# Scores of a sink-window attention: each head in its own half of the array, three products instead of four

## The chip, the cores and the metric

The kernel runs on one core of a Trainium2 chip. The engines are TensorE (PE for its matmuls, PEld for its weight loads), VectorE (DVE), ScalarE (ACT), GpSimd (POOL) and SyncE (SP, which issues all transfers here). The metric is device time in microseconds (us) of one execution. Before the change it is 691.01 us, the median of three runs (689.49 to 691.43).

## The reference

Attention with four sink positions and a window of 128, then two dense layers with a squared ReLU between them:

```python
scores = (1/sqrt(D)) * q @ k.T                     # B=4, H=8, S=768, D=64
keep   = (pos_k < n_sink) | ((rel >= 0) & (rel < window))
a      = exp(scores_kept - max) / (sum + 1e-9)
x      = (a @ v) laid out as 3072 tokens x 512
out    = (max(x @ w_in, 0) ** 2) @ w_out           # 512 -> 2048 -> 512
```

All is float32 in and out, and q and k are scaled up, so the scores are large. n_sink and window are inputs.

## The kernel before, in words

Tokens are worked in eight chunks of 384 (four batches, two halves each; NQ = 3 query blocks of 128). For each chunk there are four head pairs, so 32 pairs s = 0 to 31. `attention(s, ...)` lays down the steps of one pair: load q, k, v; scores (`score`, L477); masked reduction on VectorE (L466); exp on ScalarE (L472); reciprocal of the sums (L529, L530) and scaling on GpSimd (L537); a transposition of the probabilities; values (L726, L730). `products` (L778, L823) is the two dense layers of a chunk, 16 slices of 128 hidden units each.

A query block sees 264 keys (its own block, the one before, eight sinks), or 128 where it is the first of a sequence. One matmul loads 128 queries as weights and streams the keys.

Precision: TensorE takes F32R operands at one pass, and they carry fewer bits than F32. A number is therefore split in two parts, high and low, and products of parts are added in PSUM. The dense layers use three such products. The scores come in two kinds:

- The first eight pairs (`plain`, s < 8) multiply unsplit F32 q and k. Each head has 64 rows, head 0 in rows 0 to 63 of the array, head 1 in rows 64 to 127 (L483). The program gives each such matmul as one; the trace shows two.
- The other 24 pairs are split. For head h, `QS` holds the high part of q in 64 rows and the low part in the other 64, and `KS` holds the high part of k in all 128 rows, then the low part in all 128 rows. Two matmuls of 128 rows (L489) then add all four products. To have k in both halves of the rows it is loaded twice (`load_k`, L403), and the split is done per head: a cast of k on VectorE (L441), a subtraction on GpSimd (L446), a cast of q on ScalarE (L452) and a subtraction on VectorE (L457).

The order on every engine is fixed when the program is built. `Plan` takes all steps with an engine, a cost in us, a rank, and what they read and write, and simulates the engines: at each point it picks the step that can start first, and by rank where several can. On TensorE a step also has a mode, 0 or 1, and a change of mode adds 0.17 us to the planned cost (L126). Unsplit scores have mode 1; split scores, values and products have mode 0 (L511). Score banks come from a pool of three PSUM banks (`att`), the first layer's from two (`h`), the second's from three (`o`). The planned costs decide only the order; waits at run time are real semaphores.

Of the kernel before, what the change touches and what calls it, by code (L numbers as in the profile page):

```python
# [8 lines left out]
F32 = mybir.dt.float32  # L9
F32R = mybir.dt.float32r  # L10
# [4 lines left out]
ALU = mybir.AluOpType  # L15
# [3 lines left out]
P = 128  # L19
D = 64  # L20
NS = 8
BS = P + NS
# [23 lines left out]
def f32(ap):  # L46
    return ap.bitcast(F32)
# [107 lines left out]
def sink_window_attention_moe(  # L155
# [25 lines left out]
    with ExitStack() as fast:  # L181
# [81 lines left out]
        small = wp.tile([P, 6, 2, NQ], F32, name="small")  # L263
        sums, rcp = [small[:, i] for i in range(3)], [small[:, 3 + i] for i in range(3)]
# [13 lines left out]
        def bank(key):  # L278
            return banks[plan.got[key]]
# [80 lines left out]
        HALVES = ((0, slice(0, D), slice(D, P)), (1, slice(D, P), slice(0, D)))  # L360
# [22 lines left out]
        def attention(s, rank):  # L383
# [8 lines left out]
            if plain:  # L392
                qt, kt = ("qn", "kn") if room == 0 else (f"QS{room - 1}", f"KS{room - 1}")
            else:
                qt, kt = "qn", "kn"
            qn = lambda: sb(qt, [P, TOK], F32, f"qn_{s}")
            kn = lambda: sb(kt, [P, 2, 4, BS], F32, f"kn_{s}")
            vn, sm, rs = vns[s % 2], sums[s % 3], rcp[s % 3]
            q_cell, k_cell, v_cell, sm_cell, rs_cell = qt, kt, ("vn", s % 2), ("sm", s % 3), ("rs", s % 3)

            src = k[b, 2 * p : 2 * p + 2, :, kb0 : kb0 + nk].rearrange("h d n c -> d h (n c)")

            def load_k(a):  # L403
                h = slice(a, a + 1) if plain else slice(0, 2)
                nc.sync.dma_start(
                    out=kn()[a * D : a * D + D, h, 0:nk].rearrange("d h n c -> d h (n c)"), in_=src[:, h]
                )

            add(
                ("SP", 0.42, 2.7, 197), rank(3.2), lambda: nc.sync.dma_start(out=qn(), in_=q[b, p, :, q0 : q0 + TOK]),  # L410
                writes=[q_cell],
            )
            for a in range(2):
                add(("SP", 0.57, 4.0, 244 if not plain else 122), rank(3.2), lambda a=a: load_k(a), writes=[(k_cell, a)])
# [18 lines left out]
            KS = lambda h: sb(f"KS{h}", [P, 2, 4, BS], F32R, f"KS_{s}_{h}")  # L433
            QS = lambda h: sb(f"QS{h}", [P, TOK], F32R, f"QS_{s}_{h}")
            if not plain:
                for h, own, oth in HALVES:
                    KQ = lambda h=h: (KS(h), QS(h))
                    r = rank(2.4 - 0.5 * h)
                    add(
                        ("DVE", 0.35, "port"), r,  # L440
                        lambda h=h: nc.vector.tensor_copy(KS(h)[:, 0, 0:nk], kn()[:, h, 0:nk]),  # L441
                        reads=[(k_cell, 0), (k_cell, 1)], writes=[(f"KS{h}", 0)],
                    )
                    add(
                        ("POOL", 1.35 if nk == 4 else 1.25), r,
                        lambda h=h: nc.gpsimd.tensor_tensor(  # L446
                            KS(h)[:, 1, 0:nk], kn()[:, h, 0:nk], f32(KS(h)[:, 0, 0:nk]), op=ALU.subtract
                        ),
                        reads=[(k_cell, 0), (k_cell, 1), (f"KS{h}", 0)], writes=[(f"KS{h}", 1)],
                    )  # L450
                    add(
                        ("ACT", 0.41), r, lambda h=h, own=own: nc.scalar.copy(QS(h)[own, :], qn()[own]),  # L452
                        reads=[q_cell], writes=[f"QS{h}"],
                    )
                    add(
                        ("DVE", 0.6, "port"), r,
                        lambda h=h, own=own, oth=oth: nc.vector.tensor_tensor(  # L457
                            QS(h)[oth, :], qn()[own], f32(QS(h)[own, :]), op=ALU.subtract
                        ),
                        reads=[q_cell, f"QS{h}"], writes=[f"QS{h}"],  # L460
                    )
# [15 lines left out]
            def score(i, heads, c0, n, keys):  # L477
                cols = slice(i * P, (i + 1) * P)
                for h, key in zip(heads, keys):
                    if plain:  # L480
                        own = HALVES[h][1]
                        kf = kn()[:, h].rearrange("p n c -> p (n c)")
                        nc.tensor.matmul(  # L483
                            bank(key)[:, 0:n], qn()[own, cols], kf[own, c0 : c0 + n], start=True, stop=True
                        )
                    else:
                        flat = KS(h).rearrange("p a n c -> p a (n c)")
                        for a in range(2):
                            nc.tensor.matmul(  # L489
                                bank(key)[:, 0:n], QS(h)[:, cols], flat[:, a, c0 : c0 + n],  # L490
                                start=(a == 0), stop=(a == 1),
                            )
# [7 lines left out]
            order = [(i, (0, 1)) for i in range(NQ)] if plain else [(i, (h,)) for h in range(2) for i in range(NQ)]  # L500
            for m, (i, heads) in enumerate(order):
# [658 lines left out]
```

## Time and profile before

| what | value |
|---|---|
| runs before, us | 689.49, 691.01, 691.43 |
| profiled execution, us | 688.96 |
| its span, first to last instruction, us | 686.9 |
| mean granted TensorE clock | 0.991 |
| PE, PEld, DVE, ACT, POOL busy, us | 667.4, 581.1, 459.1, 375.0, 215.2 |
| split scores on TensorE (L489) | 288 matmuls, from 107.7 to 571.7 us |
| unsplit scores on TensorE (L483) | 96 matmuls in the trace, up to 68 us |

A busy time counts a matmul from its start to its modelled end, and matmuls overlap, so that it says how full an engine is but not what one instruction costs the next. The cost of a slot is read from distances between starts in the timeline. A row that groups instructions names line, engine, operation, output<-inputs, shapes and count, then busy time and mean ns of one, then the idle time before it. The four columns of a wait are the waiting instruction and its releaser, then the total us, the times and the longest.

### The profile page before, as it was taken

What the parts mean: (1) busy time and instruction counts of PE and PEld (TensorE: products, weight loads), DVE (VectorE), ACT (ScalarE), POOL (GpSimd) and SP (SyncE); (2) the same over time, 40 slices, a digit from 0 to 9 for tenths busy, and PEclk for the clock granted to TensorE, in tenths of its full rate; (3) what the DMA queues carried; (4) which work ended last, traced back from release to release, by engine and by line L of the source; (5) the groups of instructions that cost most, each with busy time, mean ns of one, the idle gap of its engine ahead of it and who ended that gap; (6) DMA issues with size and microseconds to landing.
All of it is one profiled execution on the core that took longest, in us unless ns stands there. A gap on an engine that the chain in (4) does not pass through costs nothing.

```text
span 686.9 us, 11380 instructions
## 1 busy us (share of the span) xinstructions
PE 667.4 (97%) x3722; PEld 581.1 (85%) x3722; DVE 459.1 (67%) x1194; ACT 375.0 (55%) x1073; POOL 215.2 (31%) x377
## 2 busy tenths in 40 slices
PE   4999989999999999999999999999999999999996
PEld 3667879998888888888888898888898888899985
DVE  7599999967987655676677766666776764242222
ACT  6798734355464434456666656666666565442221
POOL 4455433534544513232244323223332322000000
PEclk9799999999999999999999999999999999999999
DMA  7746455215777532466556666555557754310001
GB/s 244 220 163 203 168 192 183 84 52 157 223 245 227 154 106 93 134 207 193 155 148 184 211 188 201 170 167 174 145 169 213 223 160 114 116 51 12 0 1 51
DMA packets 58178, 104.78 MB, mean 153 GB/s; under 512 B 6208, under 2 KB 34624, under 8 KB 58112
## 3 DMA queue, kind: packets, MB, share of 16 engines
q1 hardware_dynamic: 58112, 103.98, 49.7%
q8 instruction: 31, 0.51, 0.3%
q14 instruction: 35, 0.29, 0.1%
HBM read 79.58 MB, written 24.38 MB: 151 GB/s over the span
## 4 chain that ended last, share of the span: by engine, by line
PE 90%; DVE 6%; ACT 1%; issue 1%; DMA 1%; SPq 0%; POOL 0%; DVEq 0%
PE bank L823 37%; PE bank L778 37%; PE bank L726 6%; PE bank L489 5%; PE bank L730 1%; DVE f L310 1%; PE bank L590 1%; PE bank L483 1%; DVE P L466 1%; PE bank L638 1%; DVE f L317 1%; DVE f L303 1%; DMA kn<-in_k_dram 1%; ACT w L323 0%; DVE w L327 0%
## 5 line engine op out<-in xcount | busy, mean ns | idle before, releaser
L778 PE MATMUL bank<-x,w 128*128 128x384 f32 x1536 | 303.1, 339 | 0.7 <-DVE gl L807 0.7
L778 PEld LDWEIGHTS bank<-x,w 128*128 128x128 f32 x1536 | 267.0, 188 | 9.5 <-issue 1.4
L823 PE MATMUL bank<-w,gh 128*128 128x512 f32 x768 | 242.7, 397 | 2.1 <-ACT ob L864 2.1
L823 PEld LDWEIGHTS bank<-w,gh 128*128 128x128 f32 x768 | 137.5, 188 | 21.4 <-ACT ob L864 2.4
L823 PE MATMUL bank<-w,gl 128*128 128x512 f32 x384 | 151.4, 394 | 0.0
L446 POOL TENSOR_TENSOR KS<-kn,KS 128x408 fp32r<-128x408 f32 (+1 forms) x48 | 64.9, 1352 | 225.1 <-DVE KS L441 164.2
L791 ACT ACTIVATE r<-bank 128x384 f32<-128x384 f32 x128 | 62.7, 490 | 129.3 <-PE bank L778 128.2
L472 ACT ACTIVATE P<-P,nbs 128x264 f32<-128x264 f32 (+1 forms) x192 | 94.4, 492 | 66.5 <-DVE nbs L466 65.7
L800 DVE TENSOR_TENSOR bank<-bank,r 128x384 f32<-128x384 f32 x128 | 72.1, 563 | 83.4 <-ACT r L791 83.1
L537 POOL TENSOR_SCALAR P<-P,small 128x128 f32<-128x128 f32 (+1 forms) x168 | 88.5, 543 | 71.1 <-DVE small L530 48.9
L823 PEld LDWEIGHTS bank<-w,gl 128*128 128x128 f32 x384 | 72.1, 188 | 16.6
L466 DVE CUSTOM_DVE_ANT_0 P<-bank,maskA 128x264 f32<-128x264 f32 x128 | 53.4, 426 | 45.1 <-PE bank L489 43.6
L807 DVE TENSOR_TENSOR gl<-bank,gh 128x384 fp32r<-128x384 f32 x128 | 70.9, 554 | 17.4 <-ACT gh L795 11.8
L795 ACT ACTIVATE gh<-r 128x384 fp32r<-128x384 f32 x128 | 66.7, 521 | 4.7 <-PE bank L823 2.2
L668 DVE STREAM_TRANSPOSE T<-P 128x384 f32<-128x384 f32 x96 | 45.2, 495 | 22.6 <-POOL P L537 21.7
L489 PEld LDWEIGHTS bank<-KS,QS 128*128 128x128 f32 x288 | 51.6, 188 | 6.2 <-DVE nbs L466 0.4
L489 PE MATMUL bank<-KS,QS 128*128 128x264 f32 (+1 forms) x288 | 55.4, 279 | 0.0
L742 ACT CAST x<-bank 128x384 fp32r<-128x384 f32 x32 | 15.3, 478 | 52.6 <-PE bank L730 52.4
L327 POOL TENSOR_TENSOR w<-f,w 128x512 fp32r<-128x512 f32 x19 | 27.1, 1430 | 51.4 <-ACT w L323 51.4
L726 PE MATMUL bank<-PT,vn 128*64 128x256 f32 (+1 forms) x392 | 40.6, 347 | 0.0
L726 PEld LDWEIGHTS bank<-PT,vn 128*64 128x64 f32 x392 | 25.7, 139 | 15.5 <-issue 6.7
L529 DVE TENSOR_TENSOR small<-small,eps 128x3 f32<-128x3 f32 (+1 forms) x56 | 34.5, 616 | 3.3 <-ACT P L472 2.7
(90 smaller groups left out, 575.5 us busy)
## 6 DMA issues: line engine op xcount, KB each, us to landing
raw<-in_moe_w_dram SPq DMA_DIRECT2D x32, 512.0 KB, 3.7
half<-in_moe_w_dram SPq DMA_DIRECT2D x64, 256.0 KB, 3.6
via<-T SPq DMA_DIRECT2D x48, 192.0 KB, 3.7
PT<-via SPq DMA_DIRECT2D x12, 768.0 KB, 4.4
via<-T SPq DMA_DIRECT2D x48, 160.0 KB, 4.2
PT<-via SPq DMA_DIRECT2D x12, 640.0 KB, 4.7
kn<-in_k_dram SPq DMA_DIRECT2D x24, 272.0 KB, 4.4
qn<-in_q_dram SPq DMA_DIRECT2D x32, 192.0 KB, 3.6
```

The costliest lines, as they stand in the source:

```text
L446: lambda h=h: nc.gpsimd.tensor_tensor(KS(h)[:, 1, 0:nk], kn()[:, h, 0:nk], f32(KS(h)[:, 0, 0:nk]), op=ALU.subtract),
L466: nc.vector.tensor_tensor_reduce(Pt(h)[:, i, o : o + n], ps_[:, 0:n], mask[:, 0:n], -SCALE, BIG, ALU.add, ALU.min, nb)
L472: nc.scalar.activation(Pt(h)[:, i, o : o + n], Pt(h)[:, i, o : o + n], AF.Exp, bias=nb, scale=-1.0, accum_out=sm[:, h, i : i + 1],)
L489: nc.tensor.matmul(bank(key)[:, 0:n], QS(h)[:, cols], flat[:, a, c0 : c0 + n], start=(a == 0), stop=(a == 1),)
L537: {"POOL": nc.gpsimd, "DVE": nc.vector}[engine].tensor_scalar(a, a, rs[:, h, i : i + 1], 1.0, op0=ALU.mult, op1=ALU.mult)
L726: nc.tensor.matmul(xo[h * D : h * D + D, qs[0] * P : qs[0] * P + len(qs) * P], vn[:, kk, h, :], rhs(), start=(n == 0), stop=False, skip_gr ...
L778: nc.tensor.matmul(bank(key)[:, 0:TOK], wi[fc][:, i, cc * P : (cc + 1) * P], xt[:, cc, :], start=(cc == 0 and j == 0), stop=(cc == NCC - 1 ...
L791: lambda key=key, r=r: nc.scalar.activation(r(), bank(key)[:, 0:TOK], AF.Relu),
L795: ("ACT", 0.41), n - 9, lambda gh=gh, r=r: nc.scalar.activation(gh(), r(), AF.Square),
L800: lambda key=key, r=r: nc.vector.tensor_tensor(bank(key)[:, 0:TOK], bank(key)[:, 0:TOK], r(), op=ALU.mult),
L807: lambda key=key, gh=gh, gl=gl: nc.vector.tensor_tensor(gl(), bank(key)[:, 0:TOK], f32(gh()), op=ALU.subtract),
L823: nc.tensor.matmul(bank(okey), gt()[:, ts_], wo[f][:, i, :], start=(f == f0 and j == 0), stop=(f == f1 - 1 and j == 2),)
```

## The change

Split scores keep each head in its own 64 rows, as the unsplit ones do. `QS` and `KS` become two tiles of two parts, `[:, 0]` high and `[:, 1]` low, with head 0 in rows 0 to 63 and head 1 in rows 64 to 127. k is loaded once into 128 rows, and q and k of both heads are split in one pass each. A query block's scores are three products for each head (q high with k high, q high with k low, q low with k high), the two heads alternating, in two PSUM banks. Both heads then go through one reciprocal step, and their transpositions have one rank. Split pairs get two buffers of their own for incoming q and k (`qns`, `kns`); the first kind uses one of them and the two parts of `QS` and `KS` as its three rooms.

```diff
+        qns = [wp.tile([P, TOK], F32, name=f"qn{i}") for i in range(2)]
+        kns = [wp.tile([P, 4, BS], F32, name=f"kn{i}") for i in range(2)]
...
-            for a in range(2):
-                add(("SP", 0.57, 4.0, 244 if not plain else 122), rank(3.2), lambda a=a: load_k(a), writes=[(k_cell, a)])
+            add(
+                ("SP", 0.5, 4.0, 70 * nk), rank(3.2),
+                lambda: nc.sync.dma_start(out=kn[:, 0:nk].rearrange("d n c -> d (n c)"), in_=src), writes=[k_cell],
+            )
...
-            KS = lambda h: sb(f"KS{h}", [P, 2, 4, BS], F32R, f"KS_{s}_{h}")
-            QS = lambda h: sb(f"QS{h}", [P, TOK], F32R, f"QS_{s}_{h}")
+            QS = lambda a: sb("QS", [P, 2, TOK], F32R, "q_parts")[:, a]
+            KS = lambda a: sb("KS", [P, 2, 4, BS], F32R, "k_parts")[:, a]
...
+                    ("DVE", 0.35, "port"), r, lambda: nc.vector.tensor_copy(KS(0)[:, 0:nk], kn[:, 0:nk]),
...
+                    lambda: nc.gpsimd.tensor_tensor(
+                        KS(1)[:, 0:nk], kn[:, 0:nk], f32(KS(0)[:, 0:nk]), op=ALU.subtract
+                    ),
...
+                    ("ACT", 0.41), r, lambda: nc.scalar.copy(QS(0), qn), reads=[q_cell],
...
+                    lambda: nc.vector.tensor_tensor(QS(1), qn, f32(QS(0)), op=ALU.subtract),
...
-                    else:
-                        flat = KS(h).rearrange("p a n c -> p a (n c)")
-                        for a in range(2):
-                            nc.tensor.matmul(
-                                bank(key)[:, 0:n], QS(h)[:, cols], flat[:, a, c0 : c0 + n],
-                                start=(a == 0), stop=(a == 1),
-                            )
+                ks = (kn,) if plain else (KS(0), KS(1), KS(0))
+                qs = (qn,) if plain else (QS(0), QS(0), QS(1))
+                for j, (qj, kj) in enumerate(zip(qs, ks)):
+                    kf = kj.rearrange("p n c -> p (n c)")
+                    for h, key in zip(heads, keys):
+                        own = slice(h * D, h * D + D)
+                        nc.tensor.matmul(
+                            bank(key)[:, 0:n], qj[own, cols], kf[own, c0 : c0 + n],
+                            start=(j == 0), stop=(j == len(qs) - 1),
+                        )
...
-            order = [(i, (0, 1)) for i in range(NQ)] if plain else [(i, (h,)) for h in range(2) for i in range(NQ)]
-            for m, (i, heads) in enumerate(order):
+            heads = (0, 1)
+            for i in range(NQ):
...
-                    reads, cost = [f"QS{h}", (f"KS{h}", 0), (f"KS{h}", 1)], (0.245 if n > P else 0.17)
+                    reads, cost = [(x, a) for x in ("QS", "KS") for a in range(2)], (0.4 if n > P else 0.23)
                 add(
                     ("PE", cost, 1 if plain else 0), r,
...
-            groups = ((0, 1),) if plain else ((0,), (1,))
-            for heads in groups:
+            if True:
...
                 for h in range(2):
-                    r = rank(1.3 if not plain and h == 0 else 0.9)
+                    r = rank(0.95)
```

How the order moves, at two places. First TensorE in the middle of the program, the scores of pair 20. Before, the three blocks of head 0 and then those of head 1 stand singly between products; these are the second block of head 0 and what is around it (x00 and x10 are the high and low part of the attention output, KS_20_0 and QS_20_0 the split operands of head 0):

```order
L778 MATMUL bank3_70<-x00_138,w_18_1060 128x384 x2
L778 MATMUL bank3_70<-x10_139,w_18_1060 128x384
L489 MATMUL bank2_69<-KS_20_0_3327,QS_20_0_3321 128x264 x2
L778 MATMUL bank3_70<-x00_138,w_18_1060 128x384 x2
L778 MATMUL bank3_70<-x10_139,w_18_1060 128x384
```

In the changed program the first block of the same pair (`score` is now L479, the products L765 and L810; k_parts and q_parts are the split operands of both heads):

```order
L810 MATMUL bank6_73<-w_15_957,gh_1_579 128x512 x2
L810 MATMUL bank6_73<-w_15_957,gl_1_589 128x512
L479 MATMUL bank2_69<-k_parts_959,q_parts_824 128x264
L479 MATMUL bank0_67<-k_parts_959,q_parts_824 128x264
L479 MATMUL bank2_69<-k_parts_959,q_parts_824 128x264
L479 MATMUL bank0_67<-k_parts_959,q_parts_824 128x264
L479 MATMUL bank2_69<-k_parts_959,q_parts_824 128x264
L479 MATMUL bank0_67<-k_parts_959,q_parts_824 128x264
L810 MATMUL bank5_72<-w_15_957,gh_1_579 128x512 x2
L810 MATMUL bank5_72<-w_15_957,gl_1_589 128x512
```

Six groups of two for a pair have become three groups of six. The whole order has 72 such groups, and each stands between products or transpositions that use the full array.

Second VectorE, behind the scores of the same pair. Before, the transpositions of head 0 stand among the reductions of head 1:

```order
L668 STREAM_TRANSPOSE T_20_3564<-P_20_0_3478 128x3x4x32
L466 ISA P_20_1_3547,nbs_125<-bank2_69,maskA_84 128x264
L466 ISA nbs_125 128x1
L668 STREAM_TRANSPOSE T_20_3564<-P_20_0_3478 128x2x4x32
L672 STREAM_TRANSPOSE T_20_3564<-P_20_0_3478 128x4x32
L466 ISA P_20_1_3547,nbs_125<-bank1_68,maskA_84 128x264
```

In the changed program those of both heads stand together (L787 and L794 belong to the products):

```order
L794 TENSOR_TENSOR gl_1_589<-bank3_70,gh_1_579 128x384
L655 STREAM_TRANSPOSE T_20_3498<-P_20_0_3371 128x3x4x32
L655 STREAM_TRANSPOSE T_20_3498<-P_20_0_3371 128x2x4x32
L659 STREAM_TRANSPOSE T_20_3498<-P_20_0_3371 128x4x32
L655 STREAM_TRANSPOSE T_20_3498<-P_20_1_3373 128x3x4x32
L655 STREAM_TRANSPOSE T_20_3498<-P_20_1_3373 128x2x4x32
L659 STREAM_TRANSPOSE T_20_3498<-P_20_1_3373 128x4x32
L734 TENSOR_TENSOR x11_145<-bank2_69,x01_144 128x384
L787 TENSOR_TENSOR bank4_71<-bank4_71,r_0_542 128x384
```

All six transpositions of a pair now follow one another, with the next product's L787 behind them.

More of the change, by code (lines that the diff above doesn't have):

```diff
@@ L431, in attention @@
                 Pt, P_cell = (lambda h: sb(f"P{h}", [P, NQ, BAND], F32, f"P_{s}_{h}")), (lambda h: ("P", h))
-            KS = lambda h: sb(f"KS{h}", [P, 2, 4, BS], F32R, f"KS_{s}_{h}")
-            QS = lambda h: sb(f"QS{h}", [P, TOK], F32R, f"QS_{s}_{h}")
+            QS = lambda a: sb("QS", [P, 2, TOK], F32R, "q_parts")[:, a]
+            KS = lambda a: sb("KS", [P, 2, 4, BS], F32R, "k_parts")[:, a]
             if not plain:
[L436 to L461, printed above, removed]
@@ new lines, in attention @@
+                first = s == NPS
+                r = rank(2.4)
+                add(
+                    ("DVE", 0.35, "port"), r, lambda: nc.vector.tensor_copy(KS(0)[:, 0:nk], kn[:, 0:nk]),
+                    reads=[k_cell], writes=[("KS", 0)] + [("KS", 1)] * first,
+                )
+                add(
+                    ("POOL", 1.35 if nk == 4 else 1.25), r,
+                    lambda: nc.gpsimd.tensor_tensor(
+                        KS(1)[:, 0:nk], kn[:, 0:nk], f32(KS(0)[:, 0:nk]), op=ALU.subtract
+                    ),
+                    reads=[k_cell, ("KS", 0)], writes=[("KS", 1)],
+                )
@@ L463, in reduce_ @@
+                add(
+                    ("ACT", 0.41), r, lambda: nc.scalar.copy(QS(0), qn), reads=[q_cell],
+                    writes=[("QS", 0)] + [("QS", 1)] * first,
+                )
+                add(
+                    ("DVE", 0.5, "port"), r,
+                    lambda: nc.vector.tensor_tensor(QS(1), qn, f32(QS(0)), op=ALU.subtract),
+                    reads=[q_cell, ("QS", 0)], writes=[("QS", 1)],
+                )
             def reduce_(h, i, n, o, mask, key):
@@ L554, in part_sinks @@
                     )
-            groups = ((0, 1),) if plain else ((0,), (1,))
-            for heads in groups:
-                hs = slice(heads[0], heads[-1] + 1)
-                r = rank(1.05 if plain or heads[0] else 1.45)
+            if True:
+                r = rank(1.05)
                 add(
-                    ("DVE", 0.22), r - URGE, lambda hs=hs: recip(hs),
+                    ("DVE", 0.22), r - URGE, lambda: recip(slice(0, 2)),
                     reads=[("e", s, h, i) for h in heads for i in range(NQ)], writes=[(rs_cell, h) for h in heads],
```

34 lines of the change are left out of this document (12 added, 22 removed).

## The prediction

> **What bounds the kernel now.** I read the page's busy shares first, then its chain, then the busy time by stage, the waits of TensorE in the long middle stage, and last the timeline of TensorE, because the question turns out to be what one group of matmuls costs there. From the page:
>
> ```profile
> PE 667.4 (97%) x3722; PEld 581.1 (85%) x3722; DVE 459.1 (67%) x1194; ACT 375.0 (55%) x1073; POOL 215.2 (31%) x377
> PE 90%; DVE 6%; ACT 1%; issue 1%; DMA 1%; SPq 0%; POOL 0%; DVEq 0%
> ```
>
> The four stages, each row with the busy time of PE, PEld, DVE, ACT and POOL, the granted clock and the DMA share; then the only wait of TensorE's matmuls between 107 and 572 us:
>
> ```profile
> 0.00:28.00 28.00, 17.48 (x91) 12.17 (x92) 17.77 (x81) 18.38 (x61) 13.92 (x38) 0.82 0.77 238
> 28.00:107.00 79.00, 76.64 (x467) 61.20 (x465) 75.53 (x169) 57.62 (x149) 34.28 (x46) 1.00 0.55 184
> 107.00:572.00 465.00, 464.30 (x2609) 411.05 (x2608) 330.84 (x869) 261.24 (x772) 165.15 (x288) 1.00 0.56 168
> 572.00:687.00 115.00, 108.95 (x562) 96.69 (x560) 35.01 (x78) 37.76 (x95) 1.88 (x5) 0.99 0.15 47
> PE bank L778 <- DVE gl L807: 0.7, 1, 0.7
> ```
>
> All split scores run from 107 to 572 us. There TensorE is idle for 0.7 us of 465 and waits once. VectorE is at 71%, GpSimd at 36%. So in this stage the time is the number of TensorE slots times their length, and a faster VectorE, ScalarE, GpSimd or DMA returns at most that 0.7 us. Everything the change does to TensorE's stream there goes into the end, one for one.
>
> **What a slot costs now.** Busy times overlap between matmuls, so I go by distances between starts. The timeline of TensorE, several places (start, length, instruction, count; a row merges neighbours):
>
> ```profile
> 203.42 0.41 PE L489 MATMUL bank<-KS,QS 128*128 128x264 f32 x2
> 203.66 0.68 PE L778 MATMUL bank<-x,w 128*128 128x384 f32 x3
> 209.88 2.27 PE L778 MATMUL bank<-x,w 128*128 128x384 f32 x12
> 211.99 0.39 PE L823 MATMUL bank<-w,gh 128*128 128x512 f32 x1
> 291.30 0.63 PE L823 MATMUL bank<-w,gh 128*128 128x512 f32 x2
> 291.77 0.39 PE L823 MATMUL bank<-w,gl 128*128 128x512 f32 x1
> 297.27 0.33 PE L489 MATMUL bank<-KS,QS 128*128 128x128 f32 x2
> 297.44 0.68 PE L823 MATMUL bank<-w,gh 128*128 128x512 f32 x2
> 297.96 0.39 PE L823 MATMUL bank<-w,gl 128*128 128x512 f32 x1
> L489 PE MATMUL bank<-KS,QS 128*128 128x264 f32 x240 | 48.0, 285 | 0.0
> L489 PE MATMUL bank<-KS,QS 128*128 128x128 f32 x48 | 8.1, 249 | 0.0
> ```
>
> Twelve first products take 211.99 - 209.88 = 2.11 us, 0.176 each. Two score matmuls of 264 columns take 203.66 - 203.42 = 0.24, 0.12 each. Two of 128 columns take 0.17, and the two L823 behind them 0.52 instead of 0.47: 0.22 for both, 0.11 each. The 288 score matmuls are 72 query blocks (24 head pairs of three) with four each, 60 blocks of 264 columns and 12 of 128. A block costs 4 x 0.12 = 0.48 us, or 0.44.
>
> **What the change makes of a block.** Six matmuls of 64 rows, in three pairs, one head in each half of the array. If the halves overlap, a block has three slots instead of four: 3 x 0.12 = 0.36. The trace has such pairs: the unsplit scores L483, which also use 64 rows per head, with F32 operands. Here is what surrounds them (the last five rows are narrow windows, to part the first two matmuls from the second two, and one that shows the clock at 9 us):
>
> ```profile
> 35.45 0.71 PE L483 MATMUL bank<-kn,qn 64*128 64x264 f32 x4
> 36.10 1.31 PE L778 MATMUL bank<-x,w 128*128 128x384 f32 x6
> 37.34 0.72 PE L483 MATMUL bank<-kn,qn 64*128 64x264 f32 x4
> 37.98 0.44 PE L590 MATMUL bank<-ident,PSK 128*128 128x128 f32 x2
> 38.88 0.71 PE L483 MATMUL bank<-kn,qn 64*128 64x264 f32 x4
> 39.53 0.44 PE L726 MATMUL bank<-PTS,vn 128*64 128x128 f32 x3
> 54.31 1.85 PE L778 MATMUL bank<-x,w 128*128 128x384 f32 x9
> 56.00 0.39 PE L823 MATMUL bank<-w,gh 128*128 128x512 f32 x1
> 37.34 0.49 PE L483 MATMUL bank<-kn,qn 64*128 64x264 f32 x2
> 37.66 0.39 PE L483 MATMUL bank<-kn,qn 64*128 64x264 f32 x2
> 8.99 0.39 PE L483 MATMUL bank<-kn,qn 64*128 64x264 f32 x2
> 9.22 0.60 PE L483 MATMUL bank<-kn,qn 64*128 64x264 f32 x4
> 8.90:9.50 0.60, 0.60 (x8) 0.55 (x7) 0.60 (x7) 0.32 (x2) 0.00 (x0) 1.00 1.09 328
> ```
>
> The two heads do overlap: both first matmuls stand in one row at 37.34 and the next two start 0.32 later. Inside a run of such pairs the distance is 9.22 - 8.99 = 0.23. Going in and out costs extra, in four places:
> - Before the group. Between the groups at 35.45 and 37.34 the six L778 take 1.24 us, not 6 x 0.176 = 1.06. Of the 0.18, 0.11 belongs to the exit (next point but one); 0.07 is the entry.
> - First pair of the group: 0.32 instead of 0.23, 0.09. Its weights are loaded with nothing streaming.
> - Last pair: 37.98 - 37.66 = 0.32 instead of 0.23, 0.09, before TensorE starts what follows.
> - Behind the group: the nine L778 from 54.31, which come straight after an L483 group, take 1.69, not 1.58: 0.11, again a first weight load that nothing covers.
>
> Sum 0.36 us for one trip into the 64-row shape and back. Rows of 64 columns (L726) are another shape: from L483 straight into L726 the distance is 39.53 - 38.88 = 0.65, no less than the 0.64 into the full array, though both are F32. So the price goes with the change of shape, not with the type of number. The Trainium skill, in "TensorEngine Tiling (Array Packing)", section Key Properties, says that a change of tiling mode, not merely of tile, drains TensorE; by that rule the change loses, and the trace agrees with its 0.07 and 0.09, and adds two bare weight loads.
>
> In the changed order each of the 72 blocks stands alone between full-array matmuls: 72 trips that were not there. The planner counts such a block as 0.4 us with no change of mode (its third number is 0, where unsplit scores have 1), so nothing gathers them.
>
> **The sum.**
> - 60 blocks: 0.36 + 0.36 - 0.48 = +0.24, 14.4 us.
> - 12 blocks of 128 columns: 0.33 + 0.36 - 0.44 = +0.25; I take +0.22, since part of the first load runs beside a slot that is itself bound by loading. 2.6 us.
> - Unsplit scores: 16 runs instead of 14, two more trips, 0.7 us; three more of them now border on L726 groups and share a change, about -0.16 each, -0.5.
> - One k load instead of two at the start. TensorE's matmuls wait for kn twice, 5.1 us in all and 4.6 of it the first time, so the second half's lateness is worth at most 0.5; I take -0.2. Not in the trace: what one 128-partition load takes to land; as late as the second half now, it gains nothing.
>
> ```profile
> PE bank L483 <- DMA kn<-in_k_dram: 5.1, 2, 4.6
> PE bank L823 <- ACT ob L864: 2.1, 1, 2.1
> L441 DVE CAST KS<-kn 128x544 fp32r<-128x544 f32 x24 | 10.5, 446 | 0.0
> L446 POOL TENSOR_TENSOR KS<-kn,KS 128x544 fp32r<-128x544 f32 x24 | 35.9, 1497 | 106.3 <-DVE KS L441 63.9 <-DMA half<-in_moe_w_dram 34.1 <-DMA vn<-in_v_dram 7.4
> L457 DVE TENSOR_TENSOR QS<-qn,QS 64x384 fp32r<-64x384 f32 x48 | 30.1, 627 | 2.2 <-ACT QS L452 0.8
> L529 DVE TENSOR_TENSOR small<-small,eps 128x3 f32<-128x3 f32 x48 | 32.6, 679 | 3.3 <-ACT P L472 2.7
> ```
>
> - Splitting once per pair drops 24 passes each of L441 (0.45), L457 (0.63) and L446 (1.50 for the long form), and 24 of L529 (0.68): some 42 us of VectorE and up to 36 of GpSimd. All of it lies beside TensorE, which waits 0.7 us for VectorE in that stage. I cost it at -0.3. The same goes for half the k traffic. The 2.1 us wait at the end of the first stage (for L864, where VectorE is 96% busy) I keep; it could go or double.
>
> Together +16.7 us. The profiled execution took 688.96 us, 2.1 beyond its 686.9 span: span 703.6, execution 705.7. The median of the runs is 691.01, 2.05 above that execution, so I forecast **707.7 us**.
>
> Bounds of the block, the term that decides: a 64-row pair with the split's number type isn't in the trace. At best there is no price for the change of shape, 0.36 against 0.48, 72 x -0.12 = -8.6 us. At worst the halves do not overlap, 6 x 0.12 + 0.36 = 1.08, 72 x 0.6 = +43 us. I take the L483 value since those matmuls have the same rows, columns and neighbours.
>
> **The rivals.**
> *Faster: the shape changes free of charge.* With this number type TensorE takes 64-row pairs without emptying itself, and the third slot saved decides: -8.6, -0.5 for starts and waits, 682. The Trainium skill, in "TensorEngine Tiling (Array Packing)", section Theoretical Speedup, gives up to 2x for 64 rows, with no price named there; that is this case, and no run here shows it for the split's type. For: only F32 pairs are seen. Against: the 0.07 before a group is paid behind L778, which has the split's type. The point at which it turns is 0.12 us per trip; three times that was measured.
>
> *Half price.* The drains (0.07 + 0.09) stay, but the loads are drawn forward under the running matmuls, as in full-array work. 0.36 + 0.16 - 0.48 = +0.04 per block: 694. Against: 0.09 and 0.11 bare in every group looked at.
>
> *A new wait on top.* A block now needs two of three score banks at once, and both heads' transposes stand in one row on VectorE:
>
> ```profile
> L668 DVE STREAM_TRANSPOSE T<-P 128x384 f32<-128x384 f32 x48 | 27.5, 573 | 22.6 <-POOL P L537 21.7
> L668 DVE STREAM_TRANSPOSE T<-P 128x256 f32<-128x256 f32 x48 | 20.0, 416 | 0.0
> L672 DVE STREAM_TRANSPOSE T<-P 128x128 f32<-128x128 f32 x24 | 6.6, 274 | 0.0
> ```
>
> Six of them are 2 x (0.57 + 0.42 + 0.27) = 2.5 us in which VectorE frees no bank and makes no gl. If TensorE waits 0.5 us for that in each of 24 pairs, 12 us on top: 720. Against: blocks of a pair stand some 4 us apart in the order, VectorE loses 42 us of work, and TensorE now runs slower than the planner thinks, which leaves the others ahead.
>
> **How the numbers follow.** Forecast 0.74, faster 0.10, half price 0.08, new wait 0.08. About 0.3% (2 us) is what a measurement of this kernel can tell from no change. Forecast and new wait are slower; of half price nearly all is slower, 0.01 the same; a partly free change could land near zero, another 0.01. Slower 0.89, same 0.02, faster 0.09. The forecast's own spread is 701 to 714 (0.30 to 0.43 per trip, waits of -3 to +3). The range reaches to half price on one side and part of a new wait on the other: 696 to 715.
>
> **What would show it.** In the changed profile the stage of the split scores should last some 17 us longer with TensorE still near 100% busy. Between two full-array matmuls around a block, the block's six should start in three pairs 0.11 to 0.22 apart, and the distance from the first to the next full-array start should be near 0.55, with 0.07 lost before and 0.11 behind. VectorE should drop by some 40 us to about 420, GpSimd to about 180. The last stage, from the last score to the end, should keep its 115 us. The forecast is wrong if the first pair starts without a gap behind a product, if the two heads' starts lie a slot apart, or if TensorE waits for VectorE in the middle stage.

## The result, and the profile after

The changed kernel takes 707.46 us (median of four runs, 707.03 to 707.57), the kernel before 691.22 in the runs beside it (four, 689.49 to 692.46). The ratio is 1.0242, 95% interval 1.0218 to 1.0266: slower by 2.4%. The forecast was 707.7.

The profiled execution of the changed kernel took 707.47 us, its span is 705.6. From the page, the busy shares and the chain of the end:

```profile
PE 685.6 (97%) x3866; PEld 571.4 (81%) x3866; DVE 418.7 (59%) x1100; ACT 361.8 (51%) x1041; POOL 176.7 (25%) x359
PE 92%; DVE 5%; issue 1%; DMA 0%; ACT 0%; DVEq 0%
```

TensorE is as full as before and busy 18 us longer; VectorE lost 40 us, GpSimd 38, ScalarE 13. By stage (columns as in the prediction: length, then PE, PEld, DVE, ACT, POOL, granted clock, DMA share, GB/s), the third stage now ending at 600 us:

```profile
0.00:28.00 28.00, 17.32 (x93) 12.55 (x95) 18.26 (x81) 19.15 (x63) 14.34 (x37) 0.82 0.73 255
28.00:107.00 79.00, 76.71 (x464) 60.91 (x465) 74.10 (x172) 53.40 (x136) 35.46 (x50) 1.00 0.55 184
107.00:600.00 493.00, 492.85 (x2813) 409.95 (x2812) 296.24 (x784) 256.72 (x765) 126.90 (x272) 1.00 0.49 148
600.00:705.00 105.00, 98.71 (x501) 87.97 (x500) 30.12 (x65) 32.52 (x78) 0.00 (x0) 0.98 0.11 39
```

TensorE is idle for 0.15 us of 493 there. Split scores stand from 136.5 to 587.2 us (before 107.7 to 571.7). The waits of TensorE's matmuls, the first three from 28 to 107 us, the fourth the only one from 107 to 600, and one of its weight loads, also from 107 to 600:

```profile
PE bank L765 <- ACT x L729: 1.0, 1, 1.0
PE bank L765 <- DVE x L734: 0.7, 1, 0.7
PE bank L810 <- DVE ob L851: 0.5, 1, 0.5
PE bank L765 <- DVE gl L794: 0.2, 1, 0.2
PEld bank L479 <- issue: 21.2, 60, 0.4
```

The long wait of before (2.1 us for L864) is gone, and three shorter ones add up to 2.2. The last row is the change's own mark: before 60 of the 72 blocks the loading of weights stands still for 21.2/60 = 0.35 us, and nothing that the profile shows releases it (ahead of the other 12 it stands still as long, with some engine's name beside it). The timeline of TensorE, around a block of 128 columns and one of 264:

```profile
303.79 0.39 PE L810 MATMUL bank<-w,gl 128*128 128x512 f32 x1
304.11 0.55 PE L479 MATMUL bank<-k_parts,q_parts 64*128 64x128 f32 x6
304.59 0.73 PE L810 MATMUL bank<-w,gh 128*128 128x512 f32 x2
305.16 0.39 PE L810 MATMUL bank<-w,gl 128*128 128x512 f32 x1
309.35 0.40 PE L810 MATMUL bank<-w,gl 128*128 128x512 f32 x1
309.68 0.63 PE L479 MATMUL bank<-k_parts,q_parts 64*128 64x264 f32 x6
310.24 2.38 PE L765 MATMUL bank<-x,w 128*128 128x384 f32 x12
312.45 0.39 PE L810 MATMUL bank<-w,gh 128*128 128x512 f32 x1
```

The L810 ahead of the block of 264 takes 309.68 - 309.35 = 0.33 us instead of 0.23, the block 310.24 - 309.68 = 0.56, and the twelve L765 behind it 2.21 instead of 2.11. So the last matmul before a block pays 0.10, and the first behind it 0.10. In the median over all 72 blocks the second pair starts 0.23 after the first, the third 0.12 after the second, and the next full-array matmul 0.21 after the third.

Where all of the time went is seen best by counting, for each matmul of either trace, the time from its start to the next matmul's start, and adding these up by kind:

| from a start to the next, summed, us | before | after | difference |
|---|---|---|---|
| split scores | 34.5 | 39.7 | +5.3 |
| first layer (L778, now L765) | 276.9 | 281.4 | +4.5 |
| second layer (L823, now L810) | 269.9 | 276.8 | +7.0 |
| transposes | 22.7 | 23.3 | +0.6 |
| values, unsplit scores | 71.8 | 72.0 | +0.2 |
| first to last matmul | 675.9 | 693.4 | +17.5 |

Two thirds of the loss don't stand with the scores but with their neighbours, as 0.10 before and behind each block. Of the 18.8 us by which the span grew (686.85 to 705.62), the rest is 0.3 at the start (first matmul at 4.89, before at 4.62) and 1.0 between the start of the last matmul and the end.

### The profile page after: what moved, and what is told of

It is laid out like the page before. It is cut to its first block, busy times and chain, and to the rows that moved or that the text cites. A ratio compares the mean times of both kernels' runs of the same rounds, so it can differ in the third digit from the quotient of the medians.

```text
span 705.6 us, 11365 instructions
## 1 busy us (share of the span) xinstructions
PE 685.6 (97%) x3866; PEld 571.4 (81%) x3866; DVE 418.7 (59%) x1100; ACT 361.8 (51%) x1041; POOL 176.7 (25%) x359
## 4 chain that ended last, share of the span: by engine, by line
PE 92%; DVE 5%; issue 1%; DMA 0%; ACT 0%; DVEq 0%
PE bank L765 38%; PE bank L810 37%; PE bank L479 7%; PE bank L713 6%; PE bank L717 2%; PE bank L577 1%; PE bank L625 1%; DVE P L460 1%; DVE f L312 1%; DVE f L305 1%; DVE f L319 1%; DMA pari<-in_params_dram 0%; DVE gl L794 0%; DVE bank L787 0%; DVE VS L375 0%
## 5 line engine op out<-in xcount | busy, mean ns | idle before, releaser
L765 PE MATMUL bank<-x,w 128*128 128x384 f32 x1536 | 303.7, 342 | 1.9 <-ACT x L729 1.0
L765 PEld LDWEIGHTS bank<-x,w 128*128 128x128 f32 x1536 | 267.7, 188 | 17.9 <-ACT x L729 1.4
L810 PE MATMUL bank<-w,gh 128*128 128x512 f32 x768 | 243.5, 398 | 0.5 <-DVE ob L851 0.5
L787 DVE TENSOR_TENSOR bank<-bank,r 128x384 f32<-128x384 f32 x128 | 72.1, 563 | 154.1 <-ACT r L778 153.4
L810 PEld LDWEIGHTS bank<-w,gh 128*128 128x128 f32 x768 | 139.2, 188 | 22.4 <-DVE ob L851 0.8
L810 PE MATMUL bank<-w,gl 128*128 128x512 f32 x384 | 151.4, 394 | 0.0
L778 ACT ACTIVATE r<-bank 128x384 f32<-128x384 f32 x128 | 62.9, 491 | 127.6 <-PE bank L765 126.5
L442 POOL TENSOR_TENSOR k_parts<-kn,k_parts 128x408 fp32r<-128x408 f32 (+1 forms) x24 | 33.6, 1401 | 314.8 <-issue 285.8
L526 POOL TENSOR_SCALAR P<-P,small 128x264 f32<-128x264 f32 (+1 forms) x174 | 83.4, 503 | 50.7 <-DVE small L519 46.5
L810 PEld LDWEIGHTS bank<-w,gl 128*128 128x128 f32 x384 | 72.0, 188 | 16.5
L794 DVE TENSOR_TENSOR gl<-bank,gh 128x384 fp32r<-128x384 f32 x128 | 71.0, 555 | 13.1 <-ACT gh L782 3.5
L460 DVE CUSTOM_DVE_ANT_0 P<-bank,maskA 128x264 f32<-128x264 f32 x128 | 50.5, 428 | 30.9 <-PE bank L479 30.3
L729 ACT CAST x<-bank 128x384 fp32r<-128x384 f32 x32 | 15.3, 478 | 72.3 <-PE bank L717 72.3
L479 PEld LDWEIGHTS bank<-k_parts,q_parts 64*128 64x128 f32 x432 | 30.1, 185 | 25.6 <-issue 21.2
L655 DVE STREAM_TRANSPOSE T<-P 128x384 f32<-128x384 f32 x96 | 43.4, 490 | 11.6 <-POOL P L526 11.1
L479 PE MATMUL bank<-k_parts,q_parts 64*128 64x264 f32 (+1 forms) x432 | 44.6, 311 | 0.0
L466 ACT ACTIVATION_READ_ACCUMULATOR P<-P,nbs 128x1 f32 x192 | 36.0, 187 | 0.0
```

The lines of the kernel that those rows point to most:

```text
L460: nc.vector.tensor_tensor_reduce(Pt(h)[:, i, o : o + n], ps_[:, 0:n], mask[:, 0:n], -SCALE, BIG, ALU.add, ALU.min, nb)
L466: nc.scalar.activation(Pt(h)[:, i, o : o + n], Pt(h)[:, i, o : o + n], AF.Exp, bias=nb, scale=-1.0, accum_out=sm[:, h, i : i + 1],)
L479: nc.tensor.matmul(bank(key)[:, 0:n], qj[own, cols], kf[own, c0 : c0 + n], start=(j == 0), stop=(j == len(qs) - 1),)
L526: {"POOL": nc.gpsimd, "DVE": nc.vector}[engine].tensor_scalar(a, a, rs[:, h, i : i + 1], 1.0, op0=ALU.mult, op1=ALU.mult)
L655: nc.vector.transpose(dst.rearrange("p c j b -> p j c b"), src.rearrange("p j (c b) -> p j c b", b=32))
L765: nc.tensor.matmul(bank(key)[:, 0:TOK], wi[fc][:, i, cc * P : (cc + 1) * P], xt[:, cc, :], start=(cc == 0 and j == 0), stop=(cc == NCC - 1 ...
```

## The experiments

The theory: a block pays for leaving and entering the full-array shape, about as much as its three pairs take, and nothing else in the change matters. The rivals: the halves don't overlap; the new order or a new wait does it; the relief of the other engines was worth something and hid part of the price. A ratio is always to the kernel before, run on the same chip.

**A second trip in each block, and the same matmul with no trip.** Into the changed kernel, a small full-array matmul between the first pair and the second of each split block. It writes columns that nobody reads, but its start clears the sum of the first product, so that this product is missing from head 0's scores. The time of the other steps does not depend on it.

```diff
+                    if not plain and j == 0:
+                        nc.tensor.matmul(
+                            bank(keys[0])[:, 504:512], qj[:, cols], kf[:, 0:8], start=True, stop=True,
+                            skip_group_check=True,
+                        )
```

> The changed kernel with one more matmul in each of the 72 split blocks: 128 rows, 8 columns, between the first and the second pair of 64-row matmuls, into columns of the bank that nobody reads. Theory (the change of shape is what costs): each block makes a second trip, last pair +0.09, a bare weight load 0.11, entry 0.09, first pair +0.10, so about +0.39 us per block, 72 x 0.39 = +28 us: 735. Rival (the 64-row pairs themselves are slow, the change of shape is cheap): only one more slot of at most 0.12, +8.6 us: 716. Rival (new waits behind the scores): 708 to 716.

The control puts the same matmul, with the same loss of a product, into the kernel before, where it changes no shape:

```diff
+                            if h == 0 and a == 0:
+                                nc.tensor.matmul(
+                                    bank(key)[:, 504:512], QS(h)[:, cols], flat[:, 0, 0:8], start=True, stop=True,
+                                    skip_group_check=True,
+                                )
```

> Control on the kernel before: the same 128-row, 8-column matmul between the two score matmuls of head 0 in each of the 72 blocks, where everything is full array. Theory: it costs one slot bound by its weight load, 0.11 to 0.12 us, so +7.7 to +8.6 us: 699. If an extra tiny matmul by itself cost as much as in the changed kernel (rival: the insertion and not the shape), it would be +28: 719.

The first took 734.98 us (ratio 1.0644, 1.0613 to 1.0675), 27.5 above the changed kernel, 0.38 for each of the 72. The control took 698.25 (1.0112, 1.0083 to 1.0141), 7.8 above the kernel before, 0.11 each. The timeline of TensorE with the second trip:

```profile
320.69 0.40 PE L815 MATMUL bank<-w,gl 128*128 128x512 f32 x1
321.02 0.39 PE L479 MATMUL bank<-k_parts,q_parts 64*128 64x264 f32 x2
321.33 0.27 PE L484 MATMUL bank<-k_parts,q_parts 128*128 128x8 f32 x1
321.54 0.51 PE L479 MATMUL bank<-k_parts,q_parts 64*128 64x264 f32 x4
321.98 1.32 PE L770 MATMUL bank<-x,w 128*128 128x384 f32 x6
```

And the control's:

```profile
202.77 0.28 PE L489 MATMUL bank<-KS,QS 128*128 128x264 f32 x1
202.89 0.17 PE L494 MATMUL bank<-KS,QS 128*128 128x8 f32 x1
202.92 0.37 PE L489 MATMUL bank<-KS,QS 128*128 128x264 f32 x1
203.12 2.07 PE L783 MATMUL bank<-x,w 128*128 128x384 f32 x11
```

The block with a second trip takes 0.96 instead of 0.56 us. Its first pair takes 0.31 until the next start, where it took 0.22; the small matmul takes 0.21; and the pair behind it takes 0.22 again, as if it were the first. In the control the small matmul adds 0.11. So 0.29 of the 0.40 goes with the change of shape alone; the other 0.11 is what the same small matmul costs in the control, as much as a full-array matmul of 128 columns. The price of a trip is thus measured apart from everything else in the change. The Trainium skill, "TensorEngine Tiling (Array Packing)", section Key Properties, says that changing the mode drains TensorE; that agrees with the 0.31 of a pair that would take 0.22, and with the 0.10 ahead of a block.

**Only one of the three products.** The changed kernel with q high times k high alone, so that its scores lack the low parts:

```diff
-                ks = (kn,) if plain else (KS(0), KS(1), KS(0))
-                qs = (qn,) if plain else (QS(0), QS(0), QS(1))
+                ks = (kn,) if plain else (KS(0),)
+                qs = (qn,) if plain else (QS(0),)
```

> The changed kernel with only the first of the three products (q high with k high); the other two are left out, so the scores lack their low parts. Theory: two slots less per block and the whole trip stays, -2 x 0.12 x 60 - 2 x 0.11 x 12 = -17 us: 690.5, so that two matmuls per block cost what four full-array ones cost before. Rival (the products are what costs): two thirds of a block's measured 0.77 us go, 72 x 0.51 = -37 us: 671.

It took 690.95 us (eight runs; ratio 1.0005, 0.9994 to 1.0016). Its timeline:

```profile
302.24 0.40 PE L810 MATMUL bank<-w,gl 128*128 128x512 f32 x1
302.57 0.39 PE L479 MATMUL bank<-k_parts,q_parts 64*128 64x264 f32 x2
302.89 0.61 PE L765 MATMUL bank<-x,w 128*128 128x384 f32 x2
```

A third of the changed kernel's score matmuls, and no gain on the kernel before: the trip with one pair (0.33 - 0.23 + 0.32 + 0.10 = 0.52) costs what four full-array matmuls did. The other two pairs are (707.46 - 690.95) / 72 = 0.23 us together, 0.115 each. Inside the 64-row shape a pair costs what a full-array matmul of as many columns costs. It is the way there that isn't free.

**Whether the halves overlap, in two ways.** First, head 1's second and third products left out (its scores lack the low parts), which leaves a pair and two single matmuls:

```diff
+                        if h == 1 and j > 0:
+                            continue
...
-                            start=(j == 0), stop=(j == len(qs) - 1),
+                            start=(j == 0), stop=(j == len(qs) - 1 or h == 1),
```

> The changed kernel with head 1's second and third product left out (its scores lack their low parts); head 0 keeps three. Theory (the two halves of the array work at the same time, also where head 0's and head 1's matmuls stand apart in the program): head 0's three slots stay, 706.5 to 708. Rival (halves take turns): two slots less per block, 72 x 0.23 = -17 us: 690.

It took 707.05 us (1.0234, 1.0214 to 1.0255), 0.4 less than with all six. Its timeline:

```profile
309.16 0.63 PE L481 MATMUL bank<-k_parts,q_parts 64*128 64x264 f32 x4
309.72 0.44 PE L767 MATMUL bank<-x,w 128*128 128x384 f32 x1
```

Four matmuls take 0.56 as six did: head 1's two lay wholly beside head 0's. Second, the same six matmuls with the heads one after the other, meant to take the overlap away:

```diff
-                for j, (qj, kj) in enumerate(zip(qs, ks)):
-                    kf = kj.rearrange("p n c -> p (n c)")
-                    for h, key in zip(heads, keys):
...
+                def one(j, h, key):
+                    own = slice(h * D, h * D + D)
+                    kf = ks[j].rearrange("p n c -> p (n c)")
+                    nc.tensor.matmul(
+                        bank(key)[:, 0:n], qs[j][own, cols], kf[own, c0 : c0 + n],
+                        start=(j == 0), stop=(j == len(qs) - 1),
+                    )
+
+                for h, key in zip(heads, keys):
+                    for j in range(len(qs)):
+                        one(j, h, key)
```

> The changed kernel with the three products of head 0 first and then those of head 1, instead of alternating. Theory (halves overlap when neighbours in the stream use different halves): only the last of head 0 and the first of head 1 overlap, five slots instead of three, +2 x 0.12 x 60 + 2 x 0.11 x 12 = +17 us: 724. Rival (the halves do not really overlap in the changed kernel either): no change, 707 to 708. If the array ran both halves out of order: 707 to 708 too.

It took 708.23 us (1.0257, 1.0227 to 1.0286), not 724. The edit did reach the program: its order on TensorE has three matmuls into one bank, then three into the other. But the timeline has the block of before the edit:

```profile
309.42 0.40 PE L813 MATMUL bank<-w,gl 128*128 128x512 f32 x1
309.74 0.64 PE L478 MATMUL bank<-k_parts,q_parts 64*128 64x264 f32 x6
310.31 0.44 PE L768 MATMUL bank<-x,w 128*128 128x384 f32 x1
```

Six in 0.57 us, and their starts in the trace stand in three pairs. Within a pair they are 10 ns apart in the median over all 72 blocks, and 19 at most. In program order head 1's first matmul could start only with or after head 0's third, and the six would need five slots; they took three. So TensorE started head 1's first matmul before head 0's second, which stands ahead of it in the program. The trace does not name the bank of a start, so this is read from the distances. The Trainium skill, "TensorE: Matmul & The Clock Gate", Part 3, The mechanism, says that matmuls start and end in program order with no reordering; the starts of this run differ, and they decide here. The edit therefore didn't test what it was meant to; the one before it did.

**The order alone, and the planner's numbers.** The kernel before with nothing but the change's order: both heads of a block in one step, one reciprocal step, transposes and splits of one rank, and the planned cost of such a step (0.49 or 0.46 us). k is still loaded twice and split per head, in full-array matmuls.

```diff
-            order = [(i, (0, 1)) for i in range(NQ)] if plain else [(i, (h,)) for h in range(2) for i in range(NQ)]
+            order = [(i, (0, 1)) for i in range(NQ)]
...
-            groups = ((0, 1),) if plain else ((0,), (1,))
+            groups = ((0, 1),)
...
-                    r = rank(1.3 if not plain and h == 0 else 0.9)
+                    r = rank(0.95)
```

> The kernel before with only the order of the change: both heads of a query block in one step of four full-array matmuls, one reciprocal step for both, transpositions of one rank; k loaded twice and split per head as before. Theory (the shape is the whole loss): 690 to 692.5. Rival (both heads at once in three banks, and six transpositions in a row, make TensorE wait): 697 to 707.

And the changed kernel with a planner that knows what a block takes:

```diff
-                    reads, cost = [(x, a) for x in ("QS", "KS") for a in range(2)], (0.4 if n > P else 0.23)
+                    reads, cost = [(x, a) for x in ("QS", "KS") for a in range(2)], (0.77 if n > P else 0.68)
```

> The changed kernel with the planner told what a split block costs as measured, 0.77 and 0.68 us instead of 0.4 and 0.23; nothing else. Theory (TensorE is full, its slots set the time): 706 to 709, no change beyond 1.5 us. Rival (the loss is partly an order laid out by wrong costs): 701 to 705.

The order alone took 691.48 us (ten runs; 1.0015, 1.0004 to 1.0026), about 1 us more than the kernel before. Its timeline has the four matmuls of a block in 0.49 us, and the middle stage is as full as it was:

```profile
224.25 0.65 PE L489 MATMUL bank<-KS,QS 128*128 128x264 f32 x4
224.74 0.51 PE L778 MATMUL bank<-x,w 128*128 128x384 f32 x2
107.00:572.00 465.00, 463.64 (x2604) 410.54 (x2603) 326.73 (x820) 260.70 (x770) 156.78 (x282) 1.00 0.57 168
```

Two banks at a time and six transposes in a row make no wait worth the name, even with all of VectorE's old passes. The better planner gave 707.35 us (1.0248, 1.0231 to 1.0265): nothing. So some 15 of the 16 us are left for the shape of the matmuls, together with whatever the single load and split of k and q gave back.

**The same new layout with no change of shape.** In the changed kernel, each head's parts of q go into tiles whose other 64 rows are zero. Then six full-array matmuls do what the three pairs do; k is still loaded and split once. There is one buffer for incoming q instead of two, the split of q is two passes of half the rows each, and GpSimd clears the tiles once.

```diff
-        qns = [wp.tile([P, TOK], F32, name=f"qn{i}") for i in range(2)]
+        qns = [wp.tile([P, TOK], F32, name="qn0")]
...
+            QZ = lambda: sb("QZ", [P, 2, 2, TOK], F32R, "q_parts")
...
-                        own = slice(h * D, h * D + D)
+                        own = slice(h * D, h * D + D) if plain else slice(0, P)
+                        qj = qn if plain else QZ()[:, h, (0, 0, 1)[j]]
```

> The changed kernel with its three products per head, k loaded and split once, but q written into two tiles whose other 64 rows are zero, so that every score matmul has 128 rows: six full-array slots per block, no change of shape (and one more ScalarE and VectorE pass per pair for q; one buffer for q instead of two). Theory: 6 x 0.12 = 0.72 instead of the measured 0.77 us, 0.65 instead of 0.68 for 128 columns: -0.05 x 60 - 0.03 x 12 = -3.2 us: 704.3. Rival (the loss is waits or order, not the shape): as the changed kernel or later for the two more passes, 707 to 709.

It took 708.78 us (1.0268, 1.0251 to 1.0285), 4.5 more than the theory and within the rival's 707 to 709, so the total alone does not tell them apart. The block does; from the timeline:

```profile
305.90 0.39 PE L823 MATMUL bank<-w,gl 128*128 128x512 f32 x1
306.13 0.78 PE L492 MATMUL bank<-k_parts,q_parts 128*128 128x128 f32 x6
306.75 0.45 PE L823 MATMUL bank<-w,gh 128*128 128x512 f32 x1
```

Nothing is lost before it (0.23), and six slots take 0.62, where the changed kernel's block of 128 columns takes 0.48 and 0.20 around it. Summed over all 72 blocks with their edges this is some 52 us against some 54: of the 3.2 us expected, about 2 came. More than that was lost elsewhere, most of it early. The stage from 92 to 127 us, in this kernel and then in the changed one, and last this kernel's longest wait of TensorE there:

```profile
92.00:127.00 35.00, 33.44 (x171) 29.09 (x168) 33.87 (x58) 14.41 (x28) 11.50 (x7) 1.00 0.58 195
```

```profile
92.00:127.00 35.00, 34.55 (x174) 31.11 (x173) 33.66 (x56) 15.06 (x29) 15.12 (x10) 1.00 0.55 193
```

```profile
96.88 0.45 PE L778 MATMUL bank<-x,w 128*128 128x384 f32 x1 [1.24 <-DVE x L747]
```

VectorE is at 97 and 96%. Compared at points where both have the same matmuls of every kind behind them, the padded kernel is 0.1 us ahead of the changed one at 93 us, 1.8 behind at 100 and still 1.75 behind at 128. In between lies that wait of 1.2 us for x. Just ahead of this x VectorE does the cast of a first k (1.47 us) and one of the half passes of q (0.54); the changed kernel has its first such cast at 83.7 us, out of the way. So this part of the loss is a matter of what stands where. Whether the added passes or the missing buffer moved it was not tried apart. What the run does show: in full-array matmuls six slots cost almost what the three pairs and their trip do.

**Whether the passes that the change saves were worth nothing.** The changed kernel with each of the four splitting passes done twice, the second writing the same again (one of the four is shown):

```diff
+def twice(emit):
+    emit()
+    emit()
...
-                    ("DVE", 0.35, "port"), r, lambda: nc.vector.tensor_copy(KS(0)[:, 0:nk], kn[:, 0:nk]),
+                    ("DVE", 0.35, "port"), r, lambda: twice(lambda: nc.vector.tensor_copy(KS(0)[:, 0:nk], kn[:, 0:nk])),
```

> The changed kernel with each of the four passes that split q and k of a pair done twice, so that VectorE, GpSimd and ScalarE get back the passes the change took from them (24 more of each). Theory (they lie beside a full TensorE): 706.5 to 709. Rival (the relief returned part of a larger loss): 710 to 716.

And once more, with a planner that knows it:

```diff
-                    ("DVE", 0.35, "port"), r, lambda: twice(lambda: nc.vector.tensor_copy(KS(0)[:, 0:nk], kn[:, 0:nk])),
+                    ("DVE", 0.9, "port"), r, lambda: twice(lambda: nc.vector.tensor_copy(KS(0)[:, 0:nk], kn[:, 0:nk])),
...
-                    ("POOL", 1.35 if nk == 4 else 1.25), r,
+                    ("POOL", 3.0 if nk == 4 else 2.5), r,
...
-                    ("ACT", 0.41), r, lambda: twice(lambda: nc.scalar.copy(QS(0), qn)), reads=[q_cell],
+                    ("ACT", 1.0), r, lambda: twice(lambda: nc.scalar.copy(QS(0), qn)), reads=[q_cell],
...
-                    ("DVE", 0.5, "port"), r,
+                    ("DVE", 1.2, "port"), r,
```

> The split passes done twice as in the run before, but now the planner is told their doubled lengths (0.9 and 1.2 us on VectorE, 3.0 or 2.5 on GpSimd, 1.0 on ScalarE), so that the order allows for them. Theory (the passes fit beside TensorE, and the 14 us came from an order that put scores where their operands were late): 706.5 to 710. Rival (the engines' time itself is short): 715 to 722.

The first took 721.81 us (1.0461, 1.0444 to 1.0479), the second 715.45 (1.0354, 1.0326 to 1.0381): 14 and 8 above the changed kernel, where the theory allowed 1.5 and 2.5. The first is beyond its rival too (716), the second at the near end of its rival (715). The three longest of the first one's waits of TensorE, 107 to 600 us:

```profile
PE bank L582 <- POOL PSK L544: 3.1, 6, 0.7
PE bank L815 <- DVE ob L849: 1.7, 1, 1.7
PE bank L484 <- DVE SK L592: 1.7, 1, 1.7
```

The six waits for GpSimd all lie behind 340 us, and from 340 to 578 us this run loses 5.0 us. In the second run the loss against the changed kernel, compared again at points of equal work, comes in two places: 1.8 us near 134 us, where TensorE waits 1.5 for gl, and 5.9 between 158 and 243 us. Behind that it keeps its distance. VectorE's timeline in the second place, and TensorE's in the same window with its waits in brackets, the only ones of TensorE there:

```profile
235.32 0.92 DVE L442 CAST k_parts<-kn 128x544 fp32r<-128x544 f32 x2
236.16 2.16 DVE L458 TENSOR_TENSOR q_parts<-qn,q_parts 128x384 fp32r<-128x384 f32 x2
238.25 1.01 DVE L799 TENSOR_TENSOR gl<-bank,gh 128x384 fp32r<-128x384 f32 x2
```

```profile
235.11 0.73 PE L815 MATMUL bank<-w,gh 128*128 128x512 f32 x2 [1.62 <-DVE ob L849]
238.84 1.33 PE L770 MATMUL bank<-x,w 128*128 128x384 f32 x3 [1.71 <-DVE gl L799]
```

The doubled passes, 3 us in a row, stand ahead of the gl that the second of these waits is for. Ahead of the other two waits (for ob here, for gl near 134 us) VectorE has no doubled pass; what made them late was not traced. By stretches:

```profile
236.30:243.00 6.70, 4.99 (x14) 3.59 (x13) 4.50 (x9) 1.02 (x4) 6.13 (x10) 0.50 0.52 180
340.00:600.00 260.00, 260.00 (x1482) 216.79 (x1482) 162.84 (x419) 155.66 (x492) 78.32 (x150) 1.00 0.53 157
```

From 236.3 to 243.0 us the granted clock was 0.50; in the us before it was 1.00. TensorE is busy for 5.0 of these 6.7 us, so by estimate the lower clock costs (1 - 0.5) x 5.0 = 2.5 us. With the two waits of 1.6 and 1.7 that is 5.8 of the 5.9 us. From 340 to 600 us the same doubled passes cost nothing, in an order that allows for them: the distance to the changed kernel stays at 7.4 to 7.2 us. So a pass on VectorE is free here where the order puts it into a gap, and dear where it stands ahead of gl; that the engines' time itself is short, the rival, does not fit those 260 us. Adding work is not the mirror of removing it. Whether the passes that the change did remove were free is answered by the order-alone run, which has all of them and a middle stage with 1.4 us idle in 465.

## Why the prediction was right, and where by luck

- **The bound.** Right. TensorE was idle for 0.15 us in 493, and of the 18.8 us that the span grew, 18.0 are the blocks with their edges.
- **The trip, 0.36 us.** Right in kind, in its four places, and nearly in size. Counted over all 72, a block with its edges went from 36.3 / 72 = 0.504 us (34.5 in it, of which 0.8 is one wait of the product behind; 1.8 around it) to 54.3 / 72 = 0.754 (39.7 in it, 6.9 ahead, 7.6 behind). That is +0.25 and 18.0 us in all, against +14.4 and +2.6 = 17.0. Both sides were put too low, and this partly cancels: the new blocks at 34.1 + 17.0 = 51.1 us (3.2 too little), the old ones at 60 x 0.48 + 12 x 0.44 = 34.1 (2.2 too little). The mis-sized parts of the trip are the entry (0.07 expected, 6.9 / 72 = 0.096) and the first pair, a little over its 0.09. The values came from F32 pairs; the split's type behaves the same.
- **The 12 blocks of 128 columns.** Their +0.22 was a choice. A typical one now takes 0.68 with its edges, against 0.45: +0.23.
- **One k load.** Wrong, small. The first matmul starts at 4.89 us, not earlier than 4.62; the 0.2 expected was not there.
- **Relief of the other engines, -0.3.** Right for this change: VectorE fell to 418.7 (about 420 expected), GpSimd to 176.7 (180), and the time did not follow. The runs with doubled passes show that the reason given, that all of it lies beside TensorE, holds only for passes in the places they had. The rows of two of them, and of the reciprocal step:

```profile
L442 POOL TENSOR_TENSOR k_parts<-kn,k_parts 128x544 fp32r<-128x544 f32 x12 | 18.8, 1568 | 165.7 <-issue 157.7 <-DVE k_parts L437 8.1
L453 DVE TENSOR_TENSOR q_parts<-qn,q_parts 128x384 fp32r<-128x384 f32 x24 | 14.5, 604 | 0.0
L518 DVE TENSOR_TENSOR small<-small,eps 128x6 f32<-128x6 f32 x32 | 19.8, 620 | 5.2 <-ACT P L466 4.8
```

- **The wait for L864.** Kept at 2.1 in the sum. It went, and 2.2 us of others came in its stage (L729, L734, L851), so the term held by luck.
- **The sum.** Expected +16.7 on the span, measured +18.8. The 2.1 are 1.0 in the blocks, 0.5 at the start (-0.2 expected, +0.3 found), 1.0 behind the start of the last matmul (6.3 us before, 7.3 now) and -0.4 in all the rest; the last two are not explained.
- **From span to median.** Here is the luck. I added 2.05 us because the profiled execution of before was that far below its median. The profiled execution of the changed kernel, 707.47, is its median. So a span 2.1 too short and an addition 2.05 too large cancel. By medians alone the change costs 707.46 - 691.22 = 16.2, near the 16.7; by the two traces 18.5. The kernel before varies between 688.6 and 692.5 over all its runs here, the changed one by half a microsecond; why was not looked into, and the profile of before is one of its fastest executions. One part may be the clock: behind the same wait of 2.1 us for L864 the profile of before has a granted clock of 1.00 (98 to 104 us), and that of the order-alone run, its slowest execution, 0.50 from 101.7 to 105.0.
- **The rivals.** *Shape free of charge* falls with the second trip (27.5 us for 72) and with the single product that gains nothing. *Half price* falls with the bare first loads: 0.23 to the second pair, 0.10 behind a block. *A new wait* falls with the 0.2 us of waiting in the middle stage and with the order alone. *No overlap*, the upper bound of the block, falls with head 1's products left out.
- **The signs.** The three pairs, the 0.10 on either side, VectorE and GpSimd came near to what was forecast. Two signs did not, because the order moved. The stage of the split scores was to last some 17 us longer; it lasts 587.2 - 136.5, some 451 us, against 464 before. 225 first-layer and 153 second-layer matmuls now stand ahead of the first split score, before 144 and 90; at 0.176 and 0.23 us each these are some 29 us that left the stage. The last stage was to keep its 115 us and has 118.4: 12 more first-layer matmuls stand in it (300, before 288), 2.1 us, and the end behind the last matmul is 1.0 longer.
- **The ranges.** Added straight, 0.30 to 0.43 per trip and waits of -3 to +3 us give 700 to 716, not 701 to 714; and the stated 696 does not quite reach half price's 694. Neither matters at 707.46.

## What to carry to other kernels

Price a change of the array's shape by the round trip, not by the slots it saves. Here 64-row pairs saved one slot of 0.12 us in four, and each trip cost about 0.4, so a trip would have to save more than three slots to pay; a block that stands alone among full-array matmuls can't. Look for that price with the neighbours: most of it appears as 0.1 us on the instruction before and the one behind, so that the group's own rows (34.5 to 39.7 us) show less than a third of the loss. And before calling an engine's work hidden, look at where it stands in its order: the same doubled passes cost nothing over 260 us where the order allowed for them, 5 us there where it did not, and where they stood ahead of an awaited gl TensorE stood still for 1.7 us.

## What the runs showed that I had not expected

- Matmuls of the two halves started out of program order: with three of head 0 ahead of three of head 1, the starts came in pairs some 10 ns apart and the time moved by 0.8 us of 707 (read from the distances, as said above). For this block the order in which the program gives the halves does not matter.
- Stretches at a granted clock of 0.50 came behind waits of TensorE of 1.6 to 2.1 us, and not behind all of them. In the last run it was 0.50 from 236.3 to 243.0 us, beginning between the waits of 1.6 and 1.7; in the run before it, from 242.0 to 245.2, behind one wait of 1.7; in the order-alone run, from 101.7 to 105.0, behind one of 2.1. Behind the same wait of 2.1 in the kernel before, and behind the 1.5 near 134 us, it stayed at 1.00. What decides was not found.
- A block of six full-array matmuls over zero-padded rows (0.62 for 128 columns, 0.67 with its edges) cost nearly as much as three half-array pairs with the way in and out (0.68).
